# A pre-norm attention and gated-MLP block on one core: V before the keys, transposes in row halves, a new instruction order

## The chip, the cores and the metric

The kernel runs on one NeuronCore of a Trainium2 chip. The metric is the device time of one execution in microseconds (us); smaller is better. Times before and after are medians over runs, and the profile is of one further execution.

## What is computed

One transformer block on 2048 rows of 448 features in bf16: a linear-attention layer (16 heads of 28) and a gated MLP (inner size 1792), each behind a layer norm and with a residual.

```python
def _A_ref(x, wqkv, w_phi, wo):
    qkv = (x @ wqkv).reshape(B, S, 3, H, Dh).transpose(2, 0, 3, 1, 4)
    q, k, v = qkv[0], qkv[1], qkv[2]
    pq = einsum("bhsd,hdf->bhsf", q, w_phi); pk = einsum("bhsd,hdf->bhsf", k, w_phi)
    phi_q = concat([softmax(pq), softmax(-pq)], -1); phi_k = concat([softmax(pk), softmax(-pk)], -1)
    kv = einsum("bhsf,bhsd->bhfd", phi_k, v); z = einsum("bhsf->bhf", phi_k)
    num = einsum("bhqf,bhfd->bhqd", phi_q, kv); den = einsum("bhqf,bhf->bhq", phi_q, z) + 1e-6
    return (num / den).transpose(0, 2, 1, 3).reshape(B, S, D) @ wo
def _B_ref(x, w_gate, w_up, w_down):
    return (sigmoid(x @ w_gate) * (x @ w_up)) @ w_down
h  = x + _A_ref(layernorm(x), wqkv, w_phi, wo)
h2 = h + _B_ref(layernorm(h), w_gate, w_up, w_down)
```

## The kernel before

The 2048 rows are 16 tiles of 128 rows. The kernel is a graph of named operations; each is put on one engine and waits, by semaphores, for the operations whose data or buffers it needs. Within an engine the operations run in an order written out by hand: the dictionary `ORDER` holds one list of names for each of SyncE (`sp`, which issues the DMAs), ScalarE (`act`), TensorE (`pe`), VectorE (`dve`) and GpSimd (`pool`). An operation that two engines could do goes to the engine in whose list its name stands. `PROGRAM` only sets the order in which operations are created.

The start. `x0`, `x1`, `x2`, `x4` and so on load rows of x (x0 and x1 one tile, the others two). `bst`/`agg` take mean and variance on VectorE, `pow1` the reciprocal root on GpSimd, `nm1` the negated mean, and `xn` writes the normalized tile. Tiles 0 to 3 are transposed on TensorE (`xT0` to `xT3`, four transposes of 128x128 each, L538) and copied out of PSUM by `xT0e` to `xT3e` (L531); later tiles are transposed by DMA. Meanwhile the key weights (`ld_k`) are transposed (`wT`, copies `wTe`, L599) and multiplied with the feature map (`w2m0_`, L612), so that one matrix gives the features of the keys directly; `w2e0_` copy it to SBUF. `wsp`/`wex` build the feature map in block form. `w2m1_`/`w2e1_` do the same for the queries, whose weights come by DMA transpose (`ld_q`). The groups `warm0` to `warm9` (L524) multiply zeros into a PSUM bank that nobody reads.

Most matmuls run in half-array form: the contraction is cut into 64 rows, one matmul on array rows 0 to 63 and one on rows 64 to 127, each writing a bank of its own; both are issued by the helper `both` (L309). An operation `...a` does eight, its second half `...b`, which swaps the banks, does six.

For the first four tiles, keys and V are projected by separate operations over two tiles: `ppa0`/`ppb0` and `ppa2`/`ppb2` for the keys, `vva0`/`vvb0` and `vva2`/`vvb2` for V. From tile 4 on `pva`/`pvb` does keys and V of one tile together. Of each tile, `ek` (ScalarE, L671 and L672) takes exponentials of the keys with both signs, `ss`/`rs` (VectorE, L675 and L681) their sums and reciprocals, `phi` (L685) the features, `v1` copies V, and `kva`/`kvb` add the tile to the key-value matrix. `pqa`/`pqb` with `eq` (L721) are the query features in chunks of four tiles.

The attention output. `kvz` masks the key-value matrix, `qs` sums features of the first two tiles, `num` multiplies, and `rsm`, `qq`, `b`, `c`, `rden`, `o` normalize on VectorE and GpSimd. The output tiles 0 and 1 are transposed on TensorE (`oT0`, `oT1`), later ones by DMA. `woa`/`wob` project with the output weights, `h` adds the residual, and a second layer norm gives `hn`, transposed on TensorE for tiles 0 and 1 (`hT0`, `hT1`) and by DMA after. `wwo` and `wgu` are empty operations on TensorE that only wait for weights.

The MLP. `ga`/`gb` are gate and up for one block of 128 inner features (over two tiles at first, over four later), `sig` (L925) the activation on ScalarE, `hh` (L926) the product on VectorE, which frees the two banks, `dn`/`dp`/`dm`/`dl` the down projection, `fin` the residual and `out` the store.

TensorE waits for an earlier operation of its own only where the two write the same bank from different row halves:

```python
    @staticmethod
    def crosses(p, o):
        return any(p.half.get(b, h) != h for b, h in o.half.items())
```

Of the kernel before, what the change touches and what calls it, by code (L numbers as in the profile page):

```python
# [18 lines left out]
class Graph:  # L19
# [90 lines left out]
    def emit(self, nc):  # L110
# [130 lines left out]
    ),  # L241
# [22 lines left out]
    ),  # L264
    "dve": (
# [14 lines left out]
    ),  # L280
    "pool": (
# [44 lines left out]
def build(nc, A_x, A_wqkv, A_w_phi, A_wo, B_w_gate, B_w_up, B_w_down, out):  # L326
# [10 lines left out]
    with ExitStack() as es:  # L337
# [63 lines left out]
        def bk16(i):  # L401
            return bk(i).bitcast(dt.bfloat16)
# [124 lines left out]
        for i, (n, size) in enumerate(((4, 512), (1, 512), (1, 128), (2, 128), (1, 128), (6, 128), (4, 128), (6, 128), (8, 128), (2, 128))):  # L527
            op("pe", "warm%d" % i, warm(n, size), r=["zero"], w=[B(3)])

        def evac(name, dst, src, rkey, wkey):  # L530
            op(("act", "dve"), name, (lambda e: e.copy(dst, src), lambda e: e.tensor_copy(dst, src)), r=[rkey], w=[wkey])  # L531

# [31 lines left out]
        def xnorm(t, a):  # L564
# [14 lines left out]
            if t < 4:  # L579
                pe_transpose("xT%d" % t, [xn_pad[:, s, kt * P:(kt + 1) * P] for kt in range(KT)], 6 + t % 2,  # L580
                             xnT[0][:, :, TS(t)], ("xn", s), ("xnT", t))
            else:
                op("sp", "xT%d" % t, lambda e: e.dma_start_transpose(out=xnT[t // 4][:, :, TS(t)], in_=xn_pad[:, s, :]),
                   r=[("xn", s)], w=[("xnT", t)], dma="tr", nring=64)
# [67 lines left out]
        def proj(t):  # L652
            bp, bv = t % 2, 2 + t % 2
            pairop("pva%d" % t, "pvb%d" % t, pair(bk(bp)[:, 0:D], bk(bv)[:, 0:D], x(t), x(t), wk2, wv),
                   [("xnT", t)] + W2k + wv_keys, bp, bv)

        def proj2(nm, t, b, w, r):
            pairop("%sa%d" % (nm, t), "%sb%d" % (nm, t), pair(bk(b)[:, 0:D], bk(b + 1)[:, 0:D], x(t), x(t + 1), w, w),
                   [("xnT", t), ("xnT", t + 1)] + r, b, b + 1)
# [375 lines left out]
```

## Time and profile before

| | before |
|---|---|
| median of 3 runs | 202.45 us (202.28 to 202.48) |
| profiled execution | 202.7 us |
| span of its profile | 200.8 us (1.9 us lie around it) |
| TensorE matmul busy | 195.5 us (97%) |
| VectorE busy | 132.0 us (66%) |
| ScalarE busy | 89.4 us (45%) |
| GpSimd busy | 56.2 us (28%) |
| HBM read, written | 8.34 MB, 1.84 MB |

In the profile PE is TensorE's matmuls, PEld its weight loads (which overlap them), DVE VectorE, ACT ScalarE, POOL GpSimd and SP SyncE. A row of a timeline gives start, length, engine, line, what is written and read, tile shape and count; in brackets stands how long the engine was idle before it and what ended that. Matmuls of a row overlap one another, so the step from one start to the next is their cost, not the length of one. A row of the chain gives start, length and what the end of the kernel was waiting for in that piece.

### The profile page before, as it was taken

The numbers are of one execution on the slowest core, as the hardware profiler recorded it, in microseconds if no ns is written. First come the engines' busy times: TensorE is split into PE (matmuls) and PEld (weight loads), VectorE is DVE, ScalarE is ACT, GpSimd is POOL, SyncE is SP. The second block draws the span as 40 slices with busy tenths as digits, with TensorE's granted clock in tenths as the row PEclk, the third lists the DMA queues.
The fourth block names the chain that finished last, engine by engine and source line by source line (L and its number), as shares of the span: only waits on it lengthen the run. The fifth ranks groups of instructions, "written<-read, shape, count | busy, mean of one in ns | idle before, by whom it ended". The sixth has DMA issues, their size and how long they took to land.

```text
span 200.8 us, 5854 instructions
## 1 busy us (share of the span) xinstructions
PE 195.5 (97%) x2516; PEld 114.4 (57%) x2516; DVE 132.0 (66%) x308; ACT 89.4 (45%) x174; POOL 56.2 (28%) x95
## 2 busy tenths in 40 slices
PE   7999999999999999999999999999999999999995
PEld 4835556565568778787444444555555555554443
DVE  5999999978888986576569877346332422272224
ACT  2668988898883451434232432324323212222220
POOL 5779948633343207510170110001400000000000
PEclk9999999999999999999999999999999999999999
DMA  6965346749984230360015220020312000004002
GB/s 157 316 140 129 54 83 76 221 144 302 309 206 66 52 57 15 66 82 3 0 29 124 56 42 10 20 58 26 65 38 52 0 3 2 0 3 137 0 3 91
DMA packets 32490, 16.26 MB, mean 81 GB/s; under 512 B 24720, under 2 KB 31568, under 8 KB 32464
## 3 DMA queue, kind: packets, MB, share of 16 engines
q1 hardware_dynamic: 32336, 15.86, 33.7%
q8 instruction: 20, 0.33, 0.7%
q14 instruction: 6, 0.05, 0.1%
q10 hardware_dynamic: 128, 0.03, 0.1%
HBM read 8.34 MB, written 1.84 MB: 51 GB/s over the span
## 4 chain that ended last, share of the span: by engine, by line
PE 92%; ACT 3%; DMA 2%; issue 1%; SPq 1%; DVE 0%
PE psum L309 84%; PE psum L954 5%; DMA wk_sb<-in_A_wqkv_dram 2%; ACT hhT L671 1%; ACT eq L721 1%; ACT hhT L672 1%; PE psum L524 1%; PE psum L538 1%; PE psum L612 1%; SPq L413 1%; PE psum L599 0%; ACT xnT L531 0%; ACT v L531 0%; DVE x_sb L961 0%
## 5 line engine op out<-in xcount | busy, mean ns | idle before, releaser
L309 PE MATMUL psum<-xnT,wu_sb 64*128 64x512 bf16 (+1 forms) x490 | 93.6, 333 | 0.0
L309 PE MATMUL psum<-xnT,wg_sb 64*128 64x512 bf16 (+1 forms) x490 | 93.5, 333 | 0.1
L925 ACT ACTIVATE sg_sb<-psum 128x512 bf16<-128x512 f32 x56 | 33.2, 596 | 90.1 <-PE psum L309 89.5
L926 DVE SCALAR_TENSOR_TENSOR hhT<-sg_sb,psum 128x512 bf16<-128x512 bf16 x56 | 37.7, 684 | 52.1 <-ACT sg_sb L925 51.7
L309 PEld LDWEIGHTS psum<-xnT,wg_sb 64*128 64x128 bf16 x490 | 44.6, 94 | 20.9 <-DVE hhT L926 2.5
L309 PEld LDWEIGHTS psum<-xnT,wu_sb 64*128 64x128 bf16 x490 | 44.7, 94 | 13.9
L309 PE MATMUL psum<-wd_sb,hhT 64*128 64x448 bf16 x336 | 37.3, 349 | 0.0
L309 PEld LDWEIGHTS psum<-wd_sb,hhT 64*128 64x128 bf16 x336 | 17.8, 94 | 14.2 <-DVE x_sb L836 0.5
L309 PE MATMUL psum<-Wk,xnT 64*128 64x448 bf16 x112 | 22.2, 350 | 0.5 <-ACT hhT L672 0.2
L309 PE MATMUL psum<-wv_sb,xnT 64*128 64x448 bf16 x112 | 22.3, 351 | 0.1
L810 POOL TENSOR_TENSOR o_pad<-c_sb,rden 128x448 bf16<-128x448 bf16 x11 | 10.2, 935 | 28.5 <-DVE rden L806 28.4
L675 DVE TENSOR_REDUCE ss<-hhT 128x32 f32<-128x896 bf16 x16 | 16.8, 1060 | 0.2 <-ACT hhT L672 0.2
L721 ACT ACTIVATE eq<-psum 120x1024 bf16<-120x1024 f32 x16 | 15.6, 1030 | 0.6 <-PE psum L309 0.4
L685 POOL TENSOR_TENSOR phi<-hhT,rs 128x896 bf16<-128x896 bf16 x8 | 13.6, 1710 | 5.6 <-DVE rs L681 3.4
L309 PE MATMUL psum<-xnT,Wq 64*120 64x512 bf16 x112 | 14.8, 383 | 0.3 <-ACT eq L721 0.2
L845 POOL TENSOR_SCALAR ve<-ssq 128x1 f32<-128x1 f32 x11 | 2.2, 201 | 41.8 <-ACT junk L842 41.5
L309 PE MATMUL psum<-wo_o,oT 64*128 64x448 bf16 x56 | 13.2, 350 | 0.0
L309 PE MATMUL psum<-wo_e,oT 64*128 64x448 bf16 x56 | 13.2, 349 | 0.0
L961 DVE SCALAR_TENSOR_TENSOR x_sb<-psum,x_sb 128x448 bf16<-128x448 f32 (+2 forms) x17 | 9.4, 592 | 2.9 <-PE psum L954 1.6
L954 PE MATMUL psum<-wd_sb,hhT 128*128 128x448 bf16 (+2 forms) x70 | 11.2, 316 | 0.0
L309 PEld LDWEIGHTS psum<-Wk,xnT 64*128 64x128 bf16 x112 | 7.8, 94 | 5.8 <-PE psum L309 1.0
L671 ACT ACTIVATE hhT<-psum 128x448 bf16<-128x448 f32 x16 | 8.8, 553 | 4.4 <-PE psum L309 4.2
(105 smaller groups left out, 234.4 us busy)
## 6 DMA issues: line engine op xcount, KB each, us to landing
out_dram<-x_sb SPq DMA_DIRECT2D x15, 112.0 KB, 1.8
x_sb<-in_A_x_dram SPq DMA_DIRECT2D x7, 224.0 KB, 4.2
wd_sb<-in_B_w_down_dram SPq DMA_DIRECT2D x7, 224.0 KB, 5.1
wg_sb<-in_B_w_gate_dram SPq DMA_DIRECT2D x3, 448.0 KB, 5.8
wu_sb<-in_B_w_up_dram SPq DMA_DIRECT2D x3, 448.0 KB, 5.7
wv_sb<-in_A_wqkv_dram SPq DMA_DIRECT2D x2, 224.0 KB, 4.7
wk_sb<-in_A_wqkv_dram SPq DMA_DIRECT2D x2, 196.0 KB, 4.1
wo_e<-in_A_wo_dram SPq DMA_DIRECT2D x1, 336.0 KB, 3.3
```

Of the source, the lines that this page charges most:

```text
L309: p = e.matmul(o, lhsT=w, rhs=r, start=st, stop=sp, tile_position=(row, 0))
L413: return op(eng, name, lambda e: e.dma_start(dst, src), r=r, w=w, dma="in" if eng == "sp" else "ain", nring=48 if eng == "sp" else 8, kb=kb)
L671: e.activation(ek[:, s, :, 0, :], src, ACT.Exp)
L675: op("dve", "ss%d" % t, lambda e: e.tensor_reduce(ss[:, s, :].rearrange("p (b h) -> p b h", h=2), eks.rearrange("p b (d h) -> p b h d", h= ...
L685: return e.tensor_tensor(phi[:, sp, :, :, :].rearrange("p b a n -> p (b a) n")[:, :, 0:56].rearrange("p b (d h) -> p b d h", h=2), eks.rea ...
L721: op("act", "eq%d_%d%s" % (c, i, "pm"[sg]), lambda e, sg=sg: e.activation(eq[c][:, sg, 2 * i:2 * i + 2, :].rearrange("p g n -> p (g n)"), ...
L810: return e.tensor_tensor(o_pad[:, t % NO, off:off + D].rearrange("p (h d) -> p h d", h=H), c_sb[:, t % NS, :, 0:DH], rden[:, t % NS, :][:, ...
L845: op(("pool", "dve"), "ve%d" % t, lambda e: e.tensor_scalar(ve2[:, t:t + 1], ssq2[:, t:t + 1], 1.0 / D ** 3, EPS, op0=ALU.mult, op1=ALU.ad ...
L925: op("act", "sig" + nm, lambda e: e.activation(sg_sb[:, k, 0:W], bk(bg)[:, 0:W], ACT.Tanh, scale=0.5), r=[B(bg)], w=[("sg", k)])
L926: op("dve", "hh" + nm, lambda e: e.scalar_tensor_tensor(out=dst, in0=sg_sb[:, k, 0:W].rearrange("p (f n) -> p f n", n=N), scalar=1.0, in1= ...
L954: p = e.matmul(bk(b)[:, lo:hi], lhsT=hb[:, ff, TS(t)], rhs=wd_sb[:, ff, lo:hi], start=ff == 0, stop=ff == FT - 1)
L961: op("dve", "fin%d%s" % (t, nm), lambda e: e.scalar_tensor_tensor(out=h_sb[:, t, lo:hi], in0=bk(b)[:, lo:hi], scalar=0.5, in1=h_sb[:, t, l ...
```

## The change

1. The V weights (`ld_v0`, `ld_v2`) are loaded right behind `x2`; the x loads `x4` and `x6` come after them instead of before.
2. V of tiles 0 and 1 (`vva0 vvb0`) runs ahead of their keys (`ppa0 ppb0`) on TensorE, and so do its copies `v1_1 v1_0` ahead of `ek0` on ScalarE. The transposes of tiles 2 and 3 stand between the two halves of the keys.
3. Two groups of dummy matmuls (`warm8` with eight, `warm9` with two) are gone; `warm2` and `warm3` (one and two) stand ahead of `wsp`, the others between the weight steps.
4. The transposes of tiles 2 and 3, of the attention outputs 0 and 1 and of the normalized h of tiles 0 and 1 are no longer four full-array transposes for each tile. A new function, `pair_transpose`, does both tiles in one operation of sixteen half-array transposes with 64 columns each; the low row half of both tiles goes to one bank, the high half to the other, and each of the two copies takes one row half of both tiles. The keys `("xnT", t)` and `("oT", s)` become pairs, one for each half.
5. The order of all engines is new. The late part of the lists is unchanged (on TensorE from about `num14` on). Some operations change engine: `w2e0_3`, `v1_13` and `oT1e` go from VectorE to ScalarE, `wTe3` and `oT0e` the other way; `o1`, `phi8`, `hn4`, `hn5` and `o10` go from GpSimd to VectorE, `phi6`, `hn2`, `hn3` and `o8` the other way; some small ones (`nm`, `ve`) move too. `wwo` moves behind `num4`.

```diff
 "sp":
-  x0 x1 ld_k0 ld_k2 x2 x4 x6 ld_v0 ld_v2 x8 x10 ...
+  x0 x1 ld_k0 ld_k2 x2 ld_v0 ld_v2 x4 x6 x8 x10 ...
 "act":
-  wphi wTe0 wTe2 wTe3 w2e0_0 w2e0_1 w2e0_2 par ek0 xT3e ek1 v1_0 v1_1 nm1_6 ek2 ek3 v1_2 w2e1_1 v1_3 nm1_8 w2e1_0 v1_4 ek4 ...
+  wphi nm1_1 wTe2 wTe0 w2e0_1 w2e0_0 w2e0_2 w2e0_3 v1_1 v1_0 nm1_4 xT3e ek0 ek1 nm1_6 par w2e1_0 w2e1_1 ek2 v1_2 v1_3 ek3 w2e1_3 ek4 v1_4 ...
 "pe":
-  warm0 warm1 wsp warm2 xT0 wT0 wT1 wT2 warm3 wT3 xT1 w2m0_0 w2m0_1 warm4 warm5 w2m0_3 w2m0_2 warm6 warm7
-  warm8 ppa0 ppb0 warm9 xT2 xT3 vva0 vvb0 ppa2 ppb2 vva2 seed vvb2 w2m1_0 w2m1_1 kva0 pva4 kvb0 pvb4 pva5
-  w2m1_2 w2m1_3 pvb5 kva1 pva6 kvb1 kva2 pvb6 kvb2 pva7 pqa0_0 pvb7 pva8 kva3 pvb8 kvb3 pqb0_0 ...
+  warm0 warm1 warm2 warm3 wsp xT0 wT1 warm4 wT2 wT3 wT0 warm5 xT1 w2m0_1 w2m0_3 warm6 w2m0_0 w2m0_2 warm7 vva0
+  vvb0 ppa0 xT2 ppb0 vva2 w2m1_1 w2m1_0 ppa2 ppb2 vvb2 seed w2m1_2 w2m1_3 kva0 pva4 pvb4 pva5 kvb0 pvb5 kva1
+  pva6 kvb1 kva2 pvb6 pva7 pqa0_0 pvb7 pva8 kvb2 kva3 pvb8 pqb0_0 kvb3 ...
-  ... kvb13 kva14 wwo kvb14 kva15 kvb15 qs ... pqa2_1 oT0 oT1 num3 pqb2_1 woa0 wob0 ... num5 hT1 hT0 woa2 ga0_2 ...
+  ... kvb13 kva14 kvb14 kva15 kvb15 qs ... pqa2_1 oT0 pqb2_1 num3 woa0 wob0 ... num5 hT0 woa2 ga0_2 ...
-  ... num11 ga2_10 ga2_11 dn2_4 gb2_10 gb2_11 ga2_12 ga2_13 num12 gb2_12 gb2_13 ...
+  ... num12 ga2_10 ga2_11 ga2_12 gb2_10 gb2_11 ga2_13 dn2_4 gb2_12 gb2_13 ...
 "dve":
-  ... xn0 kvzones wex xT0e wTe1 bst2 bst3 xT1e agg3 w2e0_3 agg2 bst7 bst5 bst4 xn2 agg5 agg4 agg7 bst6 xT2e agg6 ss0 ...
+  ... xn0 wex wTe1 xT0e wTe3 bst2 bst3 agg2 xT1e agg3 bst4 bst5 bst6 xn2 agg5 agg4 bst9 bst8 xT2e bst7 agg6 agg7 bst11 ss0 ...
-  ... rsm2 rden1 qq2 b2 c2 oT1e rsm3 ... b4 hn1 c4 hn0 rden4 rsm5 hT1e qq5 hT0e b5 c5 ...
+  ... rsm2 rden1 qq2 o1 b2 c2 oT0e rden2 rsm3 ... b4 c4 hn0 hn1 rden4 rsm5 qq5 hT0e hT1e b5 c5 ...
 "pool":
-  ident0 steps phipad ident zsel neghalf pow1_0 opad0 pow1_1 nm1_1 xn1 epsl0 v1ones wqpad epsr0 pow1_3 ...
+  ident0 steps phipad ident zsel neghalf opad0 wqpad epsr0 epsl0 pow1_0 v1ones pow1_1 xn1 pow1_2 nm1_3 pow1_3 ...
...
-for i, (n, size) in enumerate(((4, 512), (1, 512), (1, 128), (2, 128), (1, 128), (6, 128), (4, 128), (6, 128), (8, 128), (2, 128))):
+for i, (n, size) in enumerate(((4, 512), (1, 512), (1, 128), (2, 128), (1, 128), (6, 128), (4, 128), (6, 128))):
...
+def pair_transpose(names, srcs, banks, dst, rkeys, wkeys):
+    ps = [bk16(b)[:, 0:512] for b in banks]
+
+    def f(e):
+        for i, tile in enumerate(srcs):
+            for kt, src in enumerate(tile):
+                o = slice((i * KT + kt) * 64, (i * KT + kt + 1) * 64)
+                for h, rows in enumerate((LO, HI)):
+                    p = e.transpose(ps[h][:, o], src[rows], ident[rows, rows], tile_position=(64 * h, 0))
+        return p
+    op("pe", names[0], f, r=["ident"] + rkeys, w=[B(b) for b in banks], rows=64, half={b: h for h, b in enumerate(banks)})
+    for h in range(2):
+        evac(names[h] + "e", dst[h], ps[h].rearrange("p (t k s) -> p t k s", t=2, k=KT), B(banks[h]), [k[h] for k in wkeys])
...
+            v = xnT[0][:, :, 2 * P:4 * P].rearrange("p k (t h s) -> p h t k s", t=2, h=2)
+            pair_transpose(("xT2", "xT3"), [[xn_pad[:, u % NX, kt * P:(kt + 1) * P] for kt in range(KT)] for u in (2, 3)], (6, 7),
+                           [v[:, 0], v[:, 1]], [("xn", 2 % NX), ("xn", 3 % NX)], [XT(2), XT(3)])
...
```

More of the change, by code (lines that the diff above doesn't have):

```diff
@@ L531, in evac, with XT, OT @@
             op(("act", "dve"), name, (lambda e: e.copy(dst, src), lambda e: e.tensor_copy(dst, src)), r=[rkey], w=[wkey])
+        def XT(t):
+            return [("xnT", t, 0), ("xnT", t, 1)]
+        def OT(t):
+            return [("oT", t, 0), ("oT", t, 1)]
+        def pair_transpose(names, srcs, banks, dst, rkeys, wkeys):
[10 more added lines that the diff above has]
+                evac(names[h] + "e", dst[h], ps[h].rearrange("p (t k s) -> p t k s", t=2, k=KT), B(banks[h]), [k[h] for k in wkeys])
         def pe_transpose(name, srcs, bank, dst, rkey, wkey):
@@ L578, in xnorm @@
             op(("act", "dve", "pool"), "xn%d" % t, (fa, fd, fp), r=[("x", t), ("rst1", a), need], w=[("xn", s)])
-            if t < 4:
+            if t in (2, 3):
+                if t == 3:
+                    v = xnT[0][:, :, 2 * P:4 * P].rearrange("p k (t h s) -> p h t k s", t=2, h=2)
+                    pair_transpose(("xT2", "xT3"), [[xn_pad[:, u % NX, kt * P:(kt + 1) * P] for kt in range(KT)] for u in (2, 3)], (6, 7),
+                                   [v[:, 0], v[:, 1]], [("xn", 2 % NX), ("xn", 3 % NX)], [XT(2), XT(3)])
+            elif t < 2:
                 pe_transpose("xT%d" % t, [xn_pad[:, s, kt * P:(kt + 1) * P] for kt in range(KT)], 6 + t % 2,
-                             xnT[0][:, :, TS(t)], ("xn", s), ("xnT", t))
+                             xnT[0][:, :, TS(t)], ("xn", s), XT(t))
             else:
                 op("sp", "xT%d" % t, lambda e: e.dma_start_transpose(out=xnT[t // 4][:, :, TS(t)], in_=xn_pad[:, s, :]),
-                   r=[("xn", s)], w=[("xnT", t)], dma="tr", nring=64)
+                   r=[("xn", s)], w=[XT(t)], dma="tr", nring=64)
         for ts in ([0], [1], [2], [3], [4, 5], [6, 7], [8, 9, 10, 11], [12, 13, 14, 15]):
@@ L654, in proj @@
             pairop("pva%d" % t, "pvb%d" % t, pair(bk(bp)[:, 0:D], bk(bv)[:, 0:D], x(t), x(t), wk2, wv),
-                   [("xnT", t)] + W2k + wv_keys, bp, bv)
+                   [XT(t)] + W2k + wv_keys, bp, bv)
         def proj2(nm, t, b, w, r):
             pairop("%sa%d" % (nm, t), "%sb%d" % (nm, t), pair(bk(b)[:, 0:D], bk(b + 1)[:, 0:D], x(t), x(t + 1), w, w),
-                   [("xnT", t), ("xnT", t + 1)] + r, b, b + 1)
+                   [XT(t), XT(t + 1)] + r, b, b + 1)
         def vcopy(t):
@@ L714, in pq @@
                           lambda h, k: xnT[c][h, k, :], lambda h, k: xnT[c][h, k, :])
-            r = W2q + [("xnT", 4 * c + j) for j in range(4)]
+            r = W2q + [XT(4 * c + j) for j in range(4)]
             op("pe", "pqa%d_%d" % (c, i), f1, r=r, w=[B(b), B(b + 1)], rows=64, half={b: 0, b + 1: 1})
@@ L819, in otrans @@
             if t < 2:
-                pe_transpose("oT%d" % t, [o_pad[:, so, kt * P:(kt + 1) * P] for kt in range(KT)], 2 + t % 2, oT[:, so, :, :],
-                             ("opad", so), ("oT", so))
+                if t == 1:
+                    v = oT[:, 0:2, :, :].rearrange("p t k (h s) -> p h t k s", h=2)
+                    pair_transpose(("oT0", "oT1"), [[o_pad[:, u, kt * P:(kt + 1) * P] for kt in range(KT)] for u in (0, 1)], (2, 3),
+                                   [v[:, 0], v[:, 1]], [("opad", 0), ("opad", 1)], [OT(0), OT(1)])
             else:
                 op("sp", "oT%d" % t, lambda e: e.dma_start_transpose(out=oT[:, so, :, :], in_=o_pad[:, so, :]),
-                   r=[("opad", so)], w=[("oT", so)], dma="tr", nring=64)
+                   r=[("opad", so)], w=[OT(so)], dma="tr", nring=64)
         def resid(t, b, ha=False):
@@ L856, in resid @@
                 op("sp", "hT%d" % t, lambda e: e.dma_start_transpose(out=hnT[c][:, :, TS(t)], in_=hn_pad[:, s, :]),
-                   r=[("hn", s)], w=[("xnT", t)], dma="tr", nring=64)
+                   r=[("hn", s)], w=[XT(t)], dma="tr", nring=64)
         def htrans(t):
-            s = t % NH
-            pe_transpose("hT%d" % t, [hn_pad[:, s, kt * P:(kt + 1) * P] for kt in range(KT)], t, hnT[0][:, :, TS(t)], ("hn", s), ("xnT", t))
+            if t == 1:
+                v = hnT[0][:, :, 0:2 * P].rearrange("p k (t h s) -> p h t k s", t=2, h=2)
+                pair_transpose(("hT0", "hT1"), [[hn_pad[:, u, kt * P:(kt + 1) * P] for kt in range(KT)] for u in (0, 1)], (0, 1),
+                               [v[:, 0], v[:, 1]], [("hn", 0), ("hn", 1)], [XT(0), XT(1)])
         def wout(t):
@@ L877, in fb @@
                             xp(t, 2, HI, False) + [(bk(2)[:, 0:D], ot(t)(HI, k), wo_e[HI, k, :], False, k == 2) for k in (0, 1, 2)])
-            r = [("oT", t % NO), ("oT", (t + 1) % NO)] + wo_keys + ([("x", t), ("x", t + 1), "ident"] if ha else [])
+            r = [OT(t % NO), OT((t + 1) % NO)] + wo_keys + ([("x", t), ("x", t + 1), "ident"] if ha else [])
             op("pe", "woa%d" % t, fa, r=r, w=[B(2), B(3)], rows=64, half={2: 0, 3: 1})
@@ L889, in part @@
                 return [(bk(b)[:, 0:D], oT[h, so, k, :], w[h, k, :], first and k == ks[0], not first and k == ks[-1]) for k in ks]
-            r = [("oT", so)] + wo_keys
+            r = [OT(so)] + wo_keys
             op("pe", "woa%d" % t, lambda e: both(e, part(LO, lo, True), []), r=r, w=[B(b)], rows=64, half={b: 0})
@@ L904, in gate_up @@
             ns = slice((t0 % 4) * P, (t0 % 4) * P + N)
-            hk = [("xnT", t) for t in range(t0, t0 + n)]
+            hk = [XT(t) for t in range(t0, t0 + n)]
             two = n == 2
```

100 rows, old and new, of the table ORDER are left out of this document.

## The prediction

> **What bounds the kernel now.** I read the page's engine totals and chain first, then the chain piece by piece, then a table by stage, and last the timelines of the start and of the attention stage.
>
> ```profile
> PE 195.5 (97%) x2516; PEld 114.4 (57%) x2516; DVE 132.0 (66%) x308; ACT 89.4 (45%) x174; POOL 56.2 (28%) x95
> PE 92%; ACT 3%; DMA 2%; issue 1%; SPq 1%; DVE 0%
> 8.59:13.82 5.23, 4.92 (x56) 2.52 (x54) 5.18 (x14) 3.35 (x9) 4.32 (x9) 1.00 0.82 166
> 18.02:44.46 26.44, 26.22 (x480) 15.88 (x482) 24.97 (x48) 23.51 (x51) 17.70 (x15) 1.00 0.51 114
> 59.01:200.80 141.79, 139.30 (x1638) 80.84 (x1636) 79.09 (x184) 42.75 (x85) 19.29 (x37) 1.00 0.19 41
> ```
>
> TensorE carries 92% of the chain, but the 66% of VectorE hides stages: in the third and fourth rows (start to end, length, then busy time of PE, PEld, DVE, ACT, POOL, then granted clock) VectorE is busy 5.18 of 5.23 us and 24.97 of 26.44. Up to about 44 us a gain of TensorE has to be followed by VectorE; from 59 us on TensorE is alone, 139.30 of 141.79, with the tail inside the rest. So the change can win only before 59 us, and whatever it wins there arrives at the end undiminished unless the new order opens a wait later. The chain shows where TensorE is not doing useful work:
>
> ```profile
> 8.59 1.01 PE psum L524 x18
> ...
> 11.34 0.54 ACT hhT L671
> ...
> 13.82 0.95 PE psum L309 x8
> ...
> 16.58 0.44 ACT hhT L671
> ...
> 17.45 0.43 ACT v L531
> 17.89 0.14 issue
> ...
> 43.55 0.14 issue
> ...
> 44.12 0.05 issue
> ...
> 58.21 65.46 PE psum L309 x960
> ```
>
> From 8.59 it multiplies zeros 18 times for 1.01 us, waiting for the folded key weights; from 11.34 until matmuls take over at 13.82, and again up to 17.89, the chain runs through ScalarE, which takes the exponentials of the keys (two of 0.44 a tile, 16.58 to 17.45) and copies V (0.43). The hand-over from ScalarE back to TensorE costs 0.14 (17.89).
>
> **The start, step by step, in the old clock.** These are the rows I price it with:
>
> ```profile
> 9.56 1.74 PE L309 MATMUL psum<-Wk,xnT 64*128 64x448 bf16 x14
> 10.55 0.30 PEld L309 LDWEIGHTS psum<-Wk,xnT 64*128 64x128 bf16 x6 [0.50 <-PE psum L309]
> 18.02 0.35 PE L309 MATMUL psum<-Wk,xnT 64*128 64x448 bf16 x1 [0.18 <-ACT v L531]
> 18.21 0.35 PE L309 MATMUL psum<-Wk,xnT 64*128 64x448 bf16 x1
> 21.53 0.28 PE L309 MATMUL psum<-v,phi 64*128 64x58 bf16 x8
> 6.75 0.37 PE L599 MATMUL psum<-ident,wk_sb 112*112 112x112 bf16 x4
> 9.08 1.64 DVE L545 BATCH_NORM_STATS2 st<-x_sb 128x6 f32<-128x448 bf16 x3
> 11.78 0.42 DVE L531 COPY xnT<-psum 128x512 bf16<-128x512 bf16 x1
> 42.22 1.14 DVE L685 TENSOR_TENSOR phi<-hhT,rs 128x896 bf16<-128x896 bf16 x2
> 7.69 1.72 ACT L531 CAST Wk<-psum 128x448 bf16<-128x448 f32 x3
> 3.93 0.56 POOL L554 TENSOR_TENSOR rst<-mv,neghalf 128x1 f32<-128x1 f32 x1 [1.58 <-DVE mv L546]
> 4.05 0.94 SPq L413 DMA_DIRECT2D wv_sb<-in_A_wqkv_dram  x2
> wv_sb<-in_A_wqkv_dram SPq DMA_DIRECT2D x2, 224.0 KB, 4.7
> L503 SPq DMA_TRANSPOSE WqT<-in_A_wqkv_dram x4: 1246/1258/1264, 6.0 to 9.9; - x4
> DMA to landing us min/median/max: 3.7/4.4/5.0
> ```
>
> A pair of half-array matmuls of 448 columns takes 0.19 (18.02 to 18.21), so an operation of eight takes 0.76 and one of six 0.57. When the second half of a tile pair follows its first half at once, it waits for the first to leave the array: 9.56 to 10.55 is 0.99, 0.23 more than 0.76. A dummy of 128 columns is 1.01/18, that is 0.056.
>
> 1. V of tiles 0 and 1 can begin when their transposes are copied out. On VectorE the copy of tile 1 now stands behind the copy of a transposed key weight (ready at 7.12, the end of the row at 6.75), two statistics 0.53 apart and an aggregate, with 0.42 for the copy itself: 9.1. TensorE, after the folds (about 8.7) and the six dummies that stay (0.34), is there at the same time. The V weights are no obstacle: they move up two places in SyncE's queue, 0.47 each, to 3.1 and 3.6, and with 4.7 to landing are there by 8.3. The two x loads that they pass take their places, 8.8 and 9.2; their statistics come after 9.1 in the new VectorE order. The memsets that GpSimd now does ahead of its first reciprocal root fall into its idle 1.58 us there.
> 2. The V pair, 0.99 + 0.58, ends at 10.7. The four copies of folded key weights are now all ScalarE's (1.72 for three, so about 0.55 each, the first two as soon as their folds are done) and are done at 10.6, hidden by V by only 0.1. Keys 0.76, the joint transposes 0.25 (below), keys 0.58: 12.29. The same work stood finished before at 13.82. So 1.5 us is gained up to here; it does not survive.
> 3. V of tiles 2 and 3 waits for VectorE, whose copy of half the transposes now stands behind two more statistics: about 12.65, to 13.4. The two query folds wait for the last query transpose, issued at 9.9 and landing 3.7 later at the earliest, in old and new order alike: 13.7 to 14.2.
> 4. The keys' exponentials begin at 12.5 instead of 11.34 and, two tiles of some 0.9, release the banks at 14.36; plus 0.14 the keys of tiles 2 and 3 start at 14.50, against 13.82: 0.68 later. But V of the second pair and all four query folds have moved into waits.
> 5. From 14.50: keys 0.99 + 0.58, V 0.58, the seed 0.23, two folds with their switches 0.60, the first kv 0.12: 17.6. Tile 4 needs ScalarE's copy of V of tile 2, which ends at 17.68; with 0.14 it starts at 17.82, against 18.02.
> 6. Its two halves are now adjacent (0.23 more). Tile 6 is ready on TensorE at 20.96 but for ScalarE, which has tile 3's exponentials, a query weight copy, tile 4's exponentials and its V: 21.15 with the 0.14. Before, tile 6 started 0.11 after the row at 21.53, at 21.64. **Lead 0.50.**
>
> From there to 44 us the operations are the same. One kv stands between the halves of tile 8 instead of alone, where it covers a wait that was there anyway: 0.11. The empty operation that waits for the output weights leaves the last kv pairs, where the hand-over took 0.14 against 0.05 at the next one: 0.08. **Lead 0.69 at 44 us.** The engine queued behind it, VectorE, gives up one weight copy and one V copy (about 0.57 each, as ScalarE's) for a bf16 copy (0.42): about 0.7 less work, so it can just follow a lead of 0.69. Its last phi ends at 43.36 and the last kv pair starts after 43.69, so there is 0.3 besides. ScalarE gets those copies; with 23.51 busy of 26.44 it has 2.9 free.
>
> **The joint transposes.**
>
> ```profile
> 24.07 1.03 PE L309 MATMUL psum<-xnT,Wq 64*120 64x512 bf16 x8
> 24.94 0.35 PE L309 MATMUL psum<-wv_sb,xnT 64*128 64x448 bf16 x1
> 49.19 1.07 PE L309 MATMUL psum<-xnT,Wq 64*120 64x512 bf16 x8 [0.25 <-ACT eq L721]
> 50.20 0.62 PE L538 MATMUL psum<-ident,o_pad 128*128 128x128 bf16 x8
> 50.75 0.40 PE L309 MATMUL psum<-kvz,eq 56*128 56x60 bf16 x16
> 50.99 0.84 PE L309 MATMUL psum<-xnT,Wq 64*120 64x512 bf16 x6
> 48.47 1.83 POOL L810 TENSOR_TENSOR o_pad<-c_sb,rden 128x448 bf16<-128x448 bf16 x2 [6.24 <-DVE rden L806]
> 49.31 0.64 DVE L801 TENSOR_TENSOR b_sb<-psum,qq 128x464 bf16<-128x464 f32 x1
> 50.86 0.42 DVE L531 COPY oT<-psum 128x512 bf16<-128x512 bf16 x1 [0.23 <-PE psum L538]
> 66.72 0.62 DVE L810 TENSOR_TENSOR o_pad<-c_sb,rden 128x448 bf16<-128x448 bf16 x1
> ```
>
> Eight query matmuls take 0.87 (24.07 to 24.94) when more half-array work follows, and 1.01 (49.19 to 50.20) when full-array transposes follow; the transposes themselves hold 0.55 until the next half-array matmul (50.20 to 50.75). The new form is sixteen half-array matmuls of 64 columns. No row shows it; the nearest is the sixteen of 60 columns at 50.75, which hold 0.24. If the two row halves did not overlap it would be about 0.47. I take 0.25, so each of three pairs frees 0.55 + 0.14 - 0.25, some 0.4 of TensorE.
>
> How much reaches the end is set by the copies (times as if nothing had been gained before). At the attention output, o1 leaves GpSimd's series of two (1.83) for VectorE (0.62), so the transposes can run right at 50.05; but o1 pushes b2, c2 and the copy behind it back by about 0.5, less the 0.37 that the copy had in waits and in TensorE being busy: copy done 51.39, output projection at 51.54 against 51.67. **0.13.** At the normalized h, VectorE's chain and TensorE arrive 0.13 earlier, the transposes end about 0.3 sooner, and the two copies, 0.42 and back to back, release gate/up at 58.61 against 59.01: **0.40 in all there**, so 0.27 more.
>
> If these copies, which now write runs of 64 elements, cost what the float32 weight copies do (0.57) rather than 0.42, these two gains shrink by 0.15 and 0.3, to nothing together; I take 0.42, the same tile and type.
>
> **Sum.** 0.50 + 0.11 + 0.08 + 0.13 + 0.27 = 1.09 us. The profiled execution took 202.7 (span 200.8, 1.9 around it), the median of the runs 202.45; I take 1.1 off the median: **201.35**. Own range of this case: 200.7 to 201.9. The upper gain, 1.75, is all freed TensorE time: three pairs at 0.4 and ten dummies at 0.056; the lower, 0.55, is 1.09 less 0.4 for dear copies and less a few tenths of ScalarE at tile 6.
>
> **Rivals.** One more row is needed, the multiplication that frees a gate/up bank:
>
> ```profile
> L926 DVE SCALAR_TENSOR_TENSOR hhT<-sg_sb,psum 128x512 bf16<-128x512 bf16 x56 | 37.7, 684 | 52.1 <-ACT sg_sb L925 51.7
> ```
>
> Hidden anyway: VectorE cannot follow, its last phi comes no earlier, and the lead of 0.69 is gone at 44 us. For it speak 24.97 busy of 26.44; against it the 0.76 less work. Left are 0.13 + 0.27: 202.05. Chance 0.14.
>
> Slower: the first exponentials are 1.15 later, and in the old order VectorE's sums over them followed at once. If VectorE cannot fill that time with statistics brought forward, every later sum, reciprocal and phi shifts by 1.15; 0.3 of that is the slack before the last kv. It decides from about 0.75 us of VectorE idle before 20 us on; at the full shift, 0.85 lost less 0.4 gained later is 202.9. Against it: I find statistics and copies for all of that gap. 0.14.
>
> New order in the MLP stage: gate/up groups are pulled ahead, and by my walk through the queues the one after num12 meets its bank's release with next to nothing left. One such miss costs up to one multiplication, 0.68, which gives 202.05, no change. Against it: VectorE had 79.09 busy of 141.79 there. 0.08.
>
> Clock: the granted clock is 1.00 in all rows above, and the dummies were there while it rose. If it fell to half over the first V and key pairs, their 14 steps of 0.19 would take 2.7 more, less 1.1: 204.0. The Trainium skill, "TensorE: Matmul & The Clock Gate", Part 4, says that transposes do not count as activity for the clock, and Part 1 that it falls after an idle window of some 3.4 us; by that page the price would be about 1.7. No gap in the new order that I work out exceeds 0.7, and V replaces the dropped dummies. 0.03.
>
> The change does nothing measurable: the lead and the copies cancel, 202.45: 0.03.
>
> **Chances and range.** Forecast 0.58, all of it faster by over 0.2% (0.4 us, about what a measurement of this kernel can tell from no change); "hidden anyway" lies on that bound and is split. Faster 0.58 + 0.07 + 0.03 for a mild form of the MLP case = 0.68, same 0.15, slower 0.17. The range 200.7 to 202.8 leaves out the clock, half of the slower case and the tail of the forecast.
>
> **What would show it.** Right: V matmuls from about 9.1 and keys at 10.7; the keys of tiles 2 and 3 near 14.5; tile 6 near 21.15; gate/up near 57.9 in the new clock; joint transposes holding about 0.25 with no gap before them; PE in the last stage still near 139.3 us busy. Wrong: VectorE idle between 12 and 20 us; the last phi still at 43.4; the joint transposes at 0.47; a wait over 0.3 between 59 and 105 us.

## The result, and the profile after

| | before | after |
|---|---|---|
| median of the runs, us | 202.46 (202.14 to 202.81, 6 runs) | 204.68 (203.18 to 206.11, 6 runs) |
| ratio after / before | | 1.0103, 95% interval 1.0071 to 1.0135 |
| profiled execution, us | 202.7 (span 200.8) | 204.0 (span 202.0) |

The kernel became 1% slower where 0.5% faster was forecast, and its runs now spread over 3 us where they spread over 0.7. From the page of the changed kernel, first engine totals (busy time, share of the span, instructions), then the line of TensorE's instruction fetches among the DMA queues (packets, MB, share of 16 engines' span), then the chain by engine:

```profile
PE 194.6 (96%) x2530; PEld 115.3 (57%) x2530; DVE 132.0 (65%) x306; ACT 90.4 (45%) x175; POOL 55.5 (27%) x96
q8 instruction: 20, 0.33, 0.7%
PE 84%; DVE 5%; SPq 4%; DMA 4%; issue 1%; POOL 0%; DVEq 0%
```

TensorE is busy 0.9 us less in a span 1.2 us longer, and its share of the chain fell from 92% to 84%: VectorE and DMA now stand in it. The table by stage of the changed kernel, in the windows of the prediction and with the attention stage between them:

```profile
8.59:13.82 5.23, 4.70 (x62) 2.19 (x59) 5.23 (x17) 4.60 (x12) 4.29 (x8) 1.00 1.31 180
18.02:44.46 26.44, 26.20 (x492) 15.86 (x494) 25.26 (x49) 24.09 (x50) 18.30 (x16) 1.00 0.48 115
44.46:59.01 14.55, 12.60 (x219) 7.21 (x214) 13.50 (x38) 12.86 (x18) 4.84 (x6) 1.00 1.13 236
```

The same stage in the kernel before:

```profile
44.46:59.01 14.55, 14.05 (x240) 8.13 (x233) 12.66 (x37) 12.91 (x18) 5.74 (x7) 1.00 1.00 264
```

The stage that lost is the third: TensorE is busy 12.60 of 14.55 us where it was busy 14.05. The first two look like before, VectorE is as full as it was, and the clock is 1.00. The chain of the changed kernel shows what stood there:

```profile
10.18 3.90 DMA WqT<-in_A_wqkv_dram
14.08 0.14 issue
14.22 0.55 PE psum L637 x8
...
53.45 0.94 POOL o_pad L835
54.41 4.83 DMA oT<-o_pad
59.24 0.14 issue
59.37 2.49 PE psum L309 x48
...
63.05 0.65 DVE c_sb L829
63.70 0.05 issue
63.75 61.13 PE psum L309 x880
```

Attention output 3 is transposed by DMA (oT3, issued at 54.41); it lands 4.83 us later, and only then can TensorE begin woa2, the output projection of tiles 2 and 3. TensorE's timeline of the changed kernel (start, duration, then in brackets the idle time before and what ended it), in the order of the forecast's steps:

```profile
9.19 1.74 PE L309 MATMUL psum<-wv_sb,xnT 64*128 64x448 bf16 x14
10.76 0.92 PE L309 MATMUL psum<-Wk,xnT 64*128 64x448 bf16 x8
11.52 0.40 PE L547 MATMUL psum<-ident,xn_pad 64*128 64x64 bf16 x16
11.75 0.74 PE L309 MATMUL psum<-Wk,xnT 64*128 64x448 bf16 x6
12.83 0.93 PE L309 MATMUL psum<-wv_sb,xnT 64*128 64x448 bf16 x8 [0.34 <-DVE xnT L531]
14.22 0.55 PE L637 MATMUL psum<-Wphi,WqT 112*128 112x112 bf16 x8 [0.46 <-DMA WqT<-in_A_wqkv_dram]
14.70 0.93 PE L309 MATMUL psum<-Wk,xnT 64*128 64x448 bf16 x8
...
50.83 0.40 PE L309 MATMUL psum<-kvz,eq 56*128 56x60 bf16 x16
...
59.37 0.35 PE L309 MATMUL psum<-wo_e,oT 64*128 64x448 bf16 x1 [1.67 <-DMA oT<-o_pad]
...
63.75 0.40 PE L309 MATMUL psum<-kvz,eq 56*128 56x60 bf16 x16 [0.15 <-DVE c_sb L829]
```

The kernel before began woa2 here:

```profile
58.14 0.36 PE L309 MATMUL psum<-wo_e,oT 64*128 64x448 bf16 x1
```

Against the profiled execution of before, by the start of the same operation in both, the changed kernel is 0.28 ahead at tile 6, 0.33 at 43 us, 0.30 at num5 and at the first transpose of h, then 1.23 behind at woa2, 1.32 behind at ga0_4, and 1.21 behind at the last matmul. Between lead and lag lies the one wait of 1.67 us, less what the shorter transposes of h had won.

Why did oT3 land so late? Two transposes, by the tile view of oT in both kernels (DMA issue, time to land):

```profile
L823 SPq DMA_TRANSPOSE oT<-o_pad x1: 1212/1212/1212, 52.6 to 52.6; - x1
DMA to landing us min/median/max: 4.2/4.2/4.2
L823 SPq DMA_TRANSPOSE oT<-o_pad x1: 1197/1197/1197, 54.3 to 54.3; - x1
DMA to landing us min/median/max: 2.9/2.9/2.9
```

```profile
L850 SPq DMA_TRANSPOSE oT<-o_pad x1: 1212/1212/1212, 52.3 to 52.3; - x1
DMA to landing us min/median/max: 6.4/6.4/6.4
L850 SPq DMA_TRANSPOSE oT<-o_pad x1: 1191/1191/1191, 54.4 to 54.4; - x1
DMA to landing us min/median/max: 4.8/4.8/4.8
```

Before (first fence), oT2 took 4.2 us and oT3 2.9, landing at 57.24 for a woa2 that began at 58.14: a slack of 0.9 that the prediction never looked at. After (second fence), issued within 0.3 us of the same times, they took 6.4 and 4.8. The quickest in either kernel takes 2.4. Two things stand on the DMA engines at that time: the loads of the MLP's weights, issued ahead of the transposes on SyncE's queue (the last, wd2, landed at 56.28 before and 56.79 after), and a fetch of TensorE's own program. The DMA view from 55.4 to 58.8 has this line in the changed kernel, and no such line in the kernel before:

```profile
q8 instruction: 1, 0.02, 4.0%
```

The packet records date it: one packet of 16 KB, from 55.46, for 2.16 us (the 4.0% of 16 engines in this window is one engine for that time). A transpose lands in 16 parts. Of oT2 one part landed at 57.38, 0.6 behind wd2 as in the kernel before, the other fifteen only from 58.55 to 58.72, and oT3 behind them. Why one packet holds fifteen parts the records do not show. By the page's line there are 20 such fetches in the execution. What differs in the program is the count of instructions: TensorE's 2516 matmuls and weight loads became 2530 of each (three joint transposes of 16 products instead of 8, ten dummies less), so the fetches fall at other moments. The Trainium skill, "Runtime: NRT & Kernel Launch", section "Instruction fetch mechanics", says that each engine's program is refilled in blocks of 16 KiB by a DMA queue of its own, and calls the cost of a block boundary mostly hidden. The size agrees (20 packets, 0.33 MB). Whether the cost stays hidden when a transfer is under way is what the wait of 1.67 puts in doubt, and the experiments below bear on it.

### The profile page after: what moved, and what is told of

It reads as the page before. It is cut to its first block, busy times and chain, and to the rows that moved or that the text cites. A ratio compares the mean times of both kernels' runs of the same rounds, so it can differ in the third digit from the quotient of the medians.

```text
span 202.0 us, 5882 instructions
## 1 busy us (share of the span) xinstructions
PE 194.6 (96%) x2530; PEld 115.3 (57%) x2530; DVE 132.0 (65%) x306; ACT 90.4 (45%) x175; POOL 55.5 (27%) x96
## 4 chain that ended last, share of the span: by engine, by line
PE 84%; DVE 5%; SPq 4%; DMA 4%; issue 1%; POOL 0%; DVEq 0%
PE psum L309 78%; PE psum L983 5%; SPq L413 3%; DMA oT<-o_pad 2%; DMA WqT<-in_A_wqkv_dram 2%; SPq L503 2%; DVE c_sb L829 2%; DVE b_sb L826 2%; PE psum L637 1%; POOL o_pad L835 0%; DVE rden L831 0%; DVE rsm L823 0%; DVE o_pad L835 0%; DVE qq L824 0%; DVE oT L531 0%
## 5 line engine op out<-in xcount | busy, mean ns | idle before, releaser
L835 POOL TENSOR_TENSOR o_pad<-c_sb,rden 128x448 bf16<-128x448 bf16 x10 | 9.4, 936 | 22.1 <-DVE rden L831 22.1
L874 POOL TENSOR_TENSOR rst<-ve,neghalf 128x1 f32<-128x1 f32 x14 | 7.8, 562 | 13.5 <-DVE ve L872 13.0
```

Source lines behind the costliest of these rows:

```text
L835: return e.tensor_tensor(o_pad[:, t % NO, off:off + D].rearrange("p (h d) -> p h d", h=H), c_sb[:, t % NS, :, 0:DH], rden[:, t % NS, :][:, ...
L874: op("pool", "pow2_%d" % t, lambda e: e.tensor_tensor(rst2[:, t:t + 1], ve2[:, t:t + 1], neghalf[:, 0:1], ALU.pow), r=[("ve2", t), "neghal ...
```

## The experiments

**1. Loads out of the way, and the two halves of the change.** Theory Q is the queue of weight loads. The edits to the changed kernel and to the kernel before:

```diff
-ld_wd0 ld_wd1 ld_wd2 oT2 oT3 ld_wd3 ld_wd4 ld_wd5 ld_wd6 oT4
+oT2 oT3 ld_wd0 ld_wd1 ld_wd2 ld_wd3 ld_wd4 ld_wd5 ld_wd6 oT4
```

> The changed kernel with the first three down-projection loads (wd0 to wd2) behind the transposes oT2 and oT3 in SyncE's queue; all else as changed. Theory Q (the loss is one wait: the transposes oT2 and oT3 sit behind the weight loads on the DMA engines, and woa2 waits for them 1.7 us): the last weight load ahead of oT2 then lands near 54.8, so oT2 lands near 55.0 instead of 58.72 and oT3 near 56.9 instead of 59.24, the step from hT0 to woa2 shrinks from 2.08 us to about 0.3, and the kernel takes 202.1 us, between 201.7 and 202.5. Rival R (the new order of the MLP stage or the state of VectorE sets the end anyway, and the wait only shows it): woa2 starts near 57.7, but the time is given back before 70 us and the kernel stays at 203.5 or more.

Measured: 203.65 (ratio 1.0051, 1.0034 to 1.0068). From its tile view, the landings of oT2 and of oT3:

```profile
DMA to landing us min/median/max: 2.9/2.9/2.9
DMA to landing us min/median/max: 3.8/3.8/3.8
```

And from TensorE's timeline of this kernel:

```profile
58.23 0.35 PE L309 MATMUL psum<-wo_e,oT 64*128 64x448 bf16 x1 [0.69 <-DMA oT<-o_pad]
67.39 0.35 PE L309 MATMUL psum<-wo_e,oT 64*128 64x448 bf16 x1 [0.76 <-DMA oT<-o_pad]
```

oT2 landed at 55.09, as theory Q has it (55.0). oT3 did not (58.10 instead of 56.9): a fetch began at 55.46 again, for 1.16 us. The wait fell from 1.67 to 0.69, and a new one of 0.76 arose before woa4: oT4 now stood behind seven loads, and a fetch from 64.81 was under way as well (one of its parts landed at 65.44, the other fifteen from 66.72). So about 1.0 of the wait went with the loads. The queue and the fetch are not parted by this edit, because the fetch too was shorter without the loads beside it, 1.16 us instead of 2.16.

> The same move of wd0 to wd2 behind oT2 and oT3, in the kernel before. Both theories: oT3 lands near 56.8 instead of 57.25, woa2 at 58.15 does not wait for it before or after, so no change: 202.45 us, within 0.2%. If this gains more than 0.4 us, the slack of 0.9 us that I read for the kernel before is wrong in most executions.

Measured: 202.66 (1.0008, 0.9996 to 1.0019): no change, as expected.

The next two split the change. before_joint puts the joint transposes alone into the kernel before (after's `pair_transpose`, before's order); after_oldT keeps the new order with the old transposes (`xT2` becomes `xT2 xT3`, `oT0` becomes `oT0 oT1`, `hT0` becomes `hT1 hT0`).

> The kernel before, with its own order and its dummies, but with the three joint pair transposes (x tiles 2 and 3, attention outputs 0 and 1, normalized h 0 and 1). What the prediction would have: nothing at the start (old order), less than 0.13 us at the attention output because o1 stays on GpSimd, about 0.27 us at the normalized h: 202.1 us. Theory C (the copies out of the joint transposes cost more than I took, or wait longer): 202.4 to 202.8. Theory Q: oT2 and oT3 stay clear of woa2 as in the kernel before, so no 1.7 us wait; if woa2 comes earlier by 0.4 the slack shrinks to 0.5.

> The changed kernel's order of all engines, with the old full-array transposes of the three pairs. Theory Q: the loads of wg, wu and wd are issued as in the changed kernel, so oT2 and oT3 land near 58 to 59 again; woa2 is ready some 0.4 to 0.8 us later than in the changed kernel because the old transposes are longer, and waits that much less: the time is about the changed kernel's, 203.5 to 205. Theory J (the joint transposes themselves cost the time): 202 to 202.5.

Measured: before_joint 204.60 (1.0109, 1.0090 to 1.0128), after_oldT 203.22 (1.0038, 1.0026 to 1.0050). Both forecasts failed. The joint transposes alone cost as much as the whole change, and the new order without them, which issues the same loads, had no wait at woa2: its fetch of that stretch began at 59.54, when oT3 was there (57.08). TensorE's timeline of before_joint:

```profile
57.93 0.35 PE L309 MATMUL psum<-wo_e,oT 64*128 64x448 bf16 x1 [0.36 <-DMA oT<-o_pad]
71.48 0.35 PE L309 MATMUL psum<-wo_e,oT 64*128 64x448 bf16 x1 [1.66 <-issue]
```

Its DMA view from 66.9 to 71.5 (the fetch queue, then a transpose and its time to land):

```profile
q8 instruction: 1, 0.02, 1.3%
oT<-o_pad SPq DMA_TRANSPOSE x1, 4.3
```

Its largest wait is in another place: 1.66 before woa6. The timeline names no releaser ("issue"), but oT7, which woa6 reads, landed at 71.39, 0.09 before it, after 4.3 us instead of 2.4, and a fetch had begun at 69.39; fifteen of the 16 parts of oT7 had landed by 69.47, the last 1.9 us later. In the kernel before the fetch of that stretch began at 70.92, when oT7 was there. That gave theory F: what costs is where the fetches fall, and any change in the number of TensorE's instructions moves them. Its rival J is that the joint form itself costs.

**2. The same work in more or fewer instructions.** For this the dummy products serve: their columns can be cut into more or fewer matmuls, and nothing else changes.

```diff
 # before_code28: kernel before, first dummy group
-((4, 512), ...
+((32, 64), ...
 # before_joint_code: before_joint, all groups, 19 fewer
-((4, 512), (1, 512), (1, 128), (2, 128), (1, 128), (6, 128), (4, 128), (6, 128), (8, 128), (2, 128))
+((4, 512), (1, 512), (1, 128), (1, 256), (1, 128), (2, 384), (1, 512), (2, 384), (2, 512), (1, 256))
```

> The kernel before with nothing changed but its first dummy group: 32 products of 64 columns instead of 4 of 512, the same columns and 28 matmuls more of TensorE's program. Theory F (TensorE's program is fetched by DMA in pieces of 16 KB, each occupies one DMA engine for about 1.1 us, and a transpose that it meets lands up to 2 us late; which transposes it meets depends on how many instructions lie ahead): the fetch that began at 58.88 (880 matmuls issued) moves to about 55 us, the one at 70.92 (1108 matmuls) to about 69.4, where the kernel with joint transposes had them; oT3 and oT7 land late, woa2 and woa6 wait, together 0.5 to 2.5 us: 203.5 to 204.7. Rival J (what costs is the joint transposes' own form, or the copies out of them): no wait, 202.5, within 0.3 us.

Measured: 205.62 (1.0174, 1.0115 to 1.0233). The kernel before, with nothing changed but the width of its dummies, became 3 us slower, more than the 204.7 that theory F allowed. Its timeline at woa2:

```profile
60.35 0.53 PE L309 MATMUL psum<-wo_e,oT 64*128 64x448 bf16 x1 [2.43 <-DMA oT<-o_pad]
```

Its chain at woa6:

```profile
73.84 1.25 issue
```

And three rows of its table by stage (start to end, length, busy times, then granted clock, DMA):

```profile
55.00:60.30 5.30, 2.83 (x42) 1.55 (x38) 4.38 (x13) 4.02 (x5) 2.04 (x3) 1.00 1.48 136
60.30:62.50 2.20, 2.15 (x16) 1.28 (x18) 0.00 (x0) 0.00 (x0) 0.00 (x0) 0.50 1.12 331
62.50:66.00 3.50, 3.50 (x68) 3.12 (x66) 1.46 (x5) 0.43 (x1) 0.94 (x1) 0.83 0.10 22
```

Both waits of theory F are there, before woa2 (2.43) and before woa6 (1.25); the fetches began at 56.39 (2.27 us long) and, in an execution by then 3.7 us late, at 73.01. In this execution, 207.71 us long, the idle 2.43 was also followed by a granted clock of 0.50, by the clock's records from 60.27 to 63.68; the other three runs had 1.00 and took 204.68 to 205.72.

> The kernel before with the joint pair transposes, as in before_joint, and its dummies of 128 columns merged into wider ones, the same columns in 19 matmuls fewer. Theory F: the fetch at 55.00 moves to about 57.0 and the one at 69.39 to about 70.8, both behind the transposes that were hit; the wait of 1.66 before woa6 goes and the wait of 0.37 before woa2 goes or stays below 0.5: 202.2, between 201.9 and 202.9. Rival J: 204.6 as before_joint.

Measured: 202.30 (0.9988, 0.9975 to 1.0001), against 204.60 for the same kernel with 19 dummies more. The fetches began at 58.12 and 70.76, oT3 landed 2.6 and oT7 2.4 us after issue, and neither woa2 nor woa6 waited. This pair speaks against J; F had said of both which way the time would go and at which operations. One row of its timeline prices the joint transposes themselves:

```profile
58.54 0.27 PE L309 MATMUL psum<-xnT,wg_sb 64*128 64x256 bf16 x1 [0.27 <-DVE xnT L531]
```

Gate/up now waits for VectorE's copy: this kernel was 0.48 ahead before the transposes of h, 0.79 at woa2, and 0.47 at gate/up. What the transposes save is lost again at once.

> The changed kernel with the down-projection loads spread out behind the transposes: wd0 to wd2 behind oT4, wd3 and wd4 behind oT6, wd5 and wd6 behind oT7. The first move (all of them ahead of oT4) brought oT2 to 55.09 but pushed oT4 behind seven loads, to 66.80. Theory Q and F together: oT2 lands near 55.0, oT4 and the later ones 2.3 to 2.5 after their issue, so nothing waits at woa4; the code fetch near 55.5 still hits oT3 (58.1), so woa2 waits about 0.8: 202.9, between 202.5 and 203.6. Q alone (no fetch involved): 202.1. If it stays at 203.7, the transposes were not what held it.

The order is now `oT2 oT3 oT4 ld_wd0 ld_wd1 ld_wd2 oT5 oT6 ld_wd3 ld_wd4 oT7 ld_wd5 ld_wd6`. Measured: 203.15 (1.0038, 1.0016 to 1.0059); a wait of 0.55 at woa2, oT2 at 55.50, oT3 at 58.10 with a fetch from 55.37. So far it is as Q and F together have it; but oT5 to oT7 took 2.7 to 4.5 us to land instead of 2.3 to 2.5, though no wait of TensorE shows there.

> The kernel before from the attention output on; up to there, about 44 us, the changed kernel's order on all engines (V first, V weights behind x2, two dummy groups dropped), with the old transposes. My forecast for this part was 0.69 less: 201.9. By the changed kernel's trace (lead 0.33 at 44 us, of which the kernel before shows as much by itself in two other executions): 202.2 to 202.6, no change. If it is slower than 203, the start itself costs time that the traces don't show.

The edit gives every operation up to the last kv pair the changed order and leaves the old one behind it. Measured: 203.55 (1.0053, 1.0033 to 1.0074), which decides little: this mixture has a wait of its own, 0.68 before num0 (in its list of waits 0.7 for ScalarE's kvz), because kvz now stands on ScalarE's queue behind two exponentials where either order has one. It lost another 0.29 before woa4, where a fetch from 64.50 met oT5 (4.5 us to land). Until num0 it was 0.36 ahead, like the other kernels with the changed start.

**3. The same test inside the changed kernel, and two tries for a better one.**

```diff
 # after_code51: changed kernel
-((4, 512), (1, 512), (1, 128), (2, 128), (1, 128), (6, 128), (4, 128), (6, 128))
+((32, 64), (8, 64), (1, 128), (2, 128), (1, 128), (12, 64), (8, 64), (12, 64))
 # after_three: also the loads of after_wd_spread, and
-gb0_3 num7 wob2
+gb0_3 wob2 num7
```

> The changed kernel with nothing altered but the widths of its dummy products: the same columns in 64-column pieces, 51 matmuls more of TensorE's program ahead of all else. Theory F: the fetch that began at 55.46 (844 matmuls issued) moves to between 51 and 52.5, ahead of the transposes; those at 65.17 and 70.86 to about 62 and 67.5, where the transposes they can meet are not yet needed. oT2 and oT3 still stand behind the weight loads and land near 57.0 and 57.4, when woa2 is ready at 57.6: its wait of 1.67 shrinks to 0.3 or less and the kernel takes 202.9, between 202.5 and 203.6. Theory Q (the weight loads ahead of them alone): no change, 204.0 to 204.7.

Measured: 202.87 (1.0022, 1.0007 to 1.0038) instead of 204.68, by dummies alone. Its timeline:

```profile
57.68 0.41 PE L547 MATMUL psum<-ident,hn_pad 64*128 64x64 bf16 x16
58.02 0.35 PE L309 MATMUL psum<-wo_e,oT 64*128 64x448 bf16 x1
```

The wait is gone, but not quite as I had put it: I expected the fetch between 51 and 52.5, and the trace has one from 49.56 and one from 54.81. The latter was over at 55.95, where the one in the changed kernel ended at 57.62, and oT2 still stood behind the loads then (it landed at 57.47, oT3 at 57.88). The moments of the fetches shift with the instruction count, but not exactly: 51 matmuls were added, and the fetches came 8 to 96 matmuls earlier in the program.

> The changed kernel with the three things mended that the traces blame: the dummies in 51 matmuls more (as in after_code51), the down-projection loads spread behind the transposes (as in after_wd_spread), and wob2 ahead of num7 in TensorE's queue as in the kernel before, because num7 waited 0.2 for VectorE's c in every execution of the changed order. If these are all that was lost: no wait over 0.1 at woa2, woa4, woa6 and num7, and 202.5, between 202.2 and 202.8. If the changed order has a further cost that no wait shows, it stays at 202.9 or more.

Measured: 203.49 (1.0054, 1.0040 to 1.0068): a miss. woa2 and num7 no longer wait, and at ga0_8 the kernel was 0.38 ahead of the first profile of before; then a fetch from 67.79 met oT7 while SyncE was issuing it (2.17 us for the issue instead of 1.19, 3.8 to land), and TensorE stood idle for 0.7 before woa6.

> The kernel before with its 128-column dummies merged into wider ones, 19 matmuls fewer, old transposes: the control for before_joint_code (202.30). If the joint transposes brought what that kernel has gained, this one stays at 202.5. If they brought nothing and the moved fetches did, it takes 202.3 as well. Theory F's other outcome: a fetch falls on hT2 near 72 and costs up to 1 us.

Measured: 202.79 (1.0012, 1.0001 to 1.0024), no wait at woa2 or woa6. By the medians the joint transposes would be worth 0.5 against this control, but its profiled execution was already 0.25 behind at the start, where before_joint_code's was 0.41 ahead, with the same instructions there but for the transposes of tiles 2 and 3. What the joint transposes are worth stays open between nothing and 0.5.

> The kernel before with the joint transposes and the merged dummies (as in before_joint_code, 202.30), the down-projection loads spread behind the transposes, and VectorE's second copy of the normalized h right behind the first instead of behind qq5 (0.17): gate/up waited 0.27 for that copy. If this wait shrinks by 0.15 and the transposes are freer of the loads: 202.1, between 201.9 and 202.4. If the copies bind in another way, 202.3.

Measured: 203.14 (1.0032, 1.0015 to 1.0049), a miss as well. The wait before gate/up shrank from 0.27 to 0.19, but in its profile 0.23 was lost before woa4 (oT5 took 4.4 us to land, with a fetch from 64.70) and 0.43 before woa6 (oT7, behind two loads, took 3.2). Another 0.70 passed at 48.87 between two matmuls of one operation, num2; the profile shows nothing that ended it. No version beat the kernel before by more than its measurement is uncertain.

## Why the prediction was wrong

| step of the prediction | forecast | measured |
|---|---|---|
| V of tiles 0 and 1; keys | 9.1; 10.7 | 9.19; 10.76 |
| joint transposes hold TensorE | 0.25 | 0.23 (11.52 to 11.75) |
| second V pair | 12.65 | 12.83 |
| query folds done by; keys of 2 and 3 | 14.2; 14.50 | 14.70; 14.70 |
| tile 6, lead there | 21.15, 0.50 | 21.36, 0.28 |
| lead at 44 us | 0.69 | 0.33 |
| gain at the attention output | 0.13 | -0.03 |
| gain at gate/up | 0.27 | none (before_joint_code); 0.07 (after_code51) |
| wait before woa2 | not considered | 1.67 |
| sum | -1.1 | +2.2 (medians) |

**The step that failed** is the sentence that what is won before 59 us "arrives at the end undiminished unless the new order opens a wait later", with no look at the transposes by DMA. The rivals asked which engine would be late; none asked which transfer would. The landings of before would have shown oT3 at 57.24, held there by the loads ahead of it (with three loads moved away, in before_wd_late, it landed at 56.40), and woa2 at 58.14. The forecast's own lead up to there, 0.82, and the 0.3 by which the transposes of h were to end sooner would have put woa2 at 57.02, ahead of its transposes. In the changed kernel oT3 landed at 59.24 and woa2 waited 1.67. And the 14 matmuls that the change adds were counted in time, not as instructions to be fetched.

**The mis-sized terms.** The lead at 44 us was half of the forecast because the query folds, moved ahead of the second keys, wait for the last query transpose: it was issued at 10.18, 0.25 later than before, and landed at 14.08; I had the folds done by 14.2 at the latest. Even the 0.33 is mostly spread: at kva14 seven executions with the old start lie between 0.41 ahead of the first profile and 0.24 behind (mean 0.17 ahead), seven with the changed start between 0.49 ahead and 0.09 behind (mean 0.31 ahead). That is 0.14 gained, not 0.69. At the attention output, o1 on VectorE pushed c2 to end at 50.77, and num3 waited for it (50.83). At gate/up VectorE's two copies bind, with qq5 between them in the old order and ahead of them in the new one: in the changed kernel they ended at 58.49 against 58.86, 0.37 earlier, of which 0.30 was the lead already there.

**The rivals.** "Hidden anyway" was nearest for the start: VectorE's last phi ended at 43.40 against 43.36, and the lead was small. "Slower" did not occur as described: VectorE was busy 7.82 of the 8 us from 12 to 20. The miss in the MLP stage occurred, at num7 and not after num12: 0.15 of idle time in each profile with num7 ahead of wob2, none in after_three, which puts it back. The clock stayed at 1.00 in the profiled execution and in three other runs, but the two slowest runs of the changed kernel, 205.55 and 206.11, had a mean granted clock of 0.992. The profiled execution of before_code28 has 0.992 too, with the half clock behind the pause at woa2; that those two runs had such a pause is likely, and no trace shows it. The four runs at 1.00 took 203.18 to 205.35, slower than before as well.

**Shown and not shown.** Shown, by changing dummies alone in three kernels (3.1 us lost, 2.3 and 1.8 won back): the time hangs on the number of TensorE's instructions. Nothing was lost at the dummies themselves in before_code28, which was 0.29 ahead at kva14; in the profiles the loss sits at woa2 and woa6, whose transposes were under way during a fetch. Shown in part: the queue of loads (after_wd_late). Not shown is why fifteen parts of a transpose come late at woa2 (changed kernel, before_code28) and only the last one at woa6 (before_joint, before_code28). What remains when this collision is gone, 0.4 in after_code51, is not settled either. Its profile has the 0.15 at num7, a wait of 1.12 for VectorE's copy at 12.88 (0.34 and 0.46 stood there in the changed kernel) and one of 0.64 at 36.27 for a transpose of x, which another of the moved fetches had met (from 33.03). And there is a difference that no view explains: the device time less the span was 1.79 to 1.91 in seven executions with the old start and 2.00 to 2.09 in seven with the changed one. That 0.1 to 0.2 stays open, as does why the runs of the changed kernel spread over 3 us; each run having its own collisions, and the half clock in two of them, would fit, but only one of its executions was profiled.

## What to carry to other kernels

When TensorE moves earlier, list the transfers that it will wait for next, with their landing times and slack: here it was 0.9 us, less than the forecast wanted to win. Count the instructions that an edit adds, not only their time: here 14 to 51 matmuls more or fewer moved the fetches of the program, and a 16 KB fetch in front of a short transfer cost up to 2 us at a place that the edit never touched. Before a small loss or gain is ascribed to an edit, run the same kernel with some dummy instructions more or fewer.

## What the runs showed of the hardware

Each execution has twenty fetches of 16 KB (nineteen in before_code19less), 0.9 to 2.3 us long. Where one met a transpose, the last of its 16 parts landed up to 2.3 us after its first (after_three, oT4). Most others need 0.1 to 0.3, with a fetch under way or not; one transpose of x near 29 us needed 0.8 to 1.1 in seven executions with no fetch under way, so the spread alone does not prove a fetch. The Trainium skill, "DMA: Bandwidth & Descriptors", section "Issuing engines are not separate DMA queues", says that DMAs started by the scalar, sync or gpsimd engine run on the same 16 DMA engines and interleave there. No run here tests that among engines, since SyncE issues the loads and transposes met here; the late parts look as if the same held for the program's own fetches. Half-array transposes of 64 columns hold TensorE 0.23 us for sixteen. A pause of 2.43 us was once followed by a clock of 0.50 for 3.4 us, a pause of 1.67 was not.
